# Top-k attention and an MLP mixer: the mask of head 0's last 192 columns goes in among the second scores, and the shared PSUM bank is split evenly

## The chip, the cores and the metric

The kernel runs on one core of one Trainium2 chip. The metric is device time in microseconds (us): the median of three runs before the change was 724.96 us (724.28 to 725.15). One further execution was taken with the hardware profiler; all rows shown here come from it.

## The reference

Eight batches of eight heads, 576 rows, head dimension 64. For each row only the 32 largest scores keep their weight:

```
scores = scale * q @ k^T                       # 576 x 576 for each head
kth    = the 32nd largest score of each row
scores = where(scores >= kth, scores, -1e9)
attn   = exp(scores - max) ; attn /= sum(attn) + 1e-9
x      = heads of attn @ v side by side        # 8 x 576 x 512
h      = relu(x^T @ w_tok1) @ w_tok2           # over the 576 rows
u      = x + h^T
out    = u + relu(u @ w_ch1) @ w_ch2
```

## The kernel before

**Tiles and engines.** Two heads are handled together (`front`, `back`, L450 and L738), in 32 such pairs. The 576 rows of a pair make four tiles of 128 and one of 64, which it shares with the next pair, so two pairs make nine tiles and the whole kernel 144 calls of `scores` (L553), one for each row tile with its two heads: head 0 lives on partitions 0 to 63 of the transposed `qT` and `kT`, head 1 on 64 to 127. For one such call:

- TensorE (PE) computes the scores of both heads, `score` (L569, matmuls at L565). ScalarE (ACT) copies them out of PSUM to `SX` as scaled integers (L598, recorded at L366).
- VectorE (DVE) finds candidates for the 32nd largest with MAX8 over six segments (L614 to L620). ACT counts how many scores lie above a guess (L632). GpSimd (POOL) and DVE turn that into the exact threshold (L640, L649).
- In 100 of the 144 calls (`swap`) POOL writes a mask byte for each score into `U` (L658). Then `rescore` (L577) has PE put mask times a tiny factor into PSUM (`excess`, L583, with `identN` as the stationary operand) and add the scores a second time on top (`second`, L589), so that one ACT instruction (L663) can take the exponential straight out of PSUM. In the other 44 calls POOL multiplies instead (L669, L673).
- `Pm` is transposed by DMA into `PT` (L695), and PE multiplies it with `v` (L754). The mixer follows batch by batch on PE and ACT (`mlp_ops`, L793; L892 and L940 are its largest matmuls).

**PSUM of one call.** The 2 x 576 f32 scores take three banks of 512 columns. Head 0 has bank 0 and the first 64 columns of bank 1, head 1 the last 64 columns of bank 1 and bank 2: `APART = 960` is the distance of the heads, `CUT` (L292) cuts head 0 at 512 and head 1 at 64.

**Row tiles.** A 64-row stationary operand uses one half of the PE array; head 0's matmuls run in one half (row tile 0) and head 1's in the other (row tile 1) at the same time. The kernel never lets the two write the same bank at once. `pieces` (L381) issues four pieces: head 1's first 64 columns (bank 1), head 0's first 512 (bank 0), head 1's last 512 (bank 2), and, behind a wait of PE on the semaphore `tiles_done` until head 1's first piece is complete, head 0's last 64 (bank 1). `score` goes through it once and `rescore` twice, first with `excess`, then with `second`. Each `excess` piece is two matmuls of 64 x 64, one for each half of the rows, so that both row tiles work on it; each `second` piece is one matmul of 64 x 128. A float32 matmul stands in the trace as two instructions.

**The order.** The whole program is a list of 6,041 operations (`plan.add`). `Plan.run` (L206) sorts them by the string `ORDER` (L32), which gives each its place, and issues each engine's own in that order; an engine's queue is not rearranged at run time. The costs in `plan.add` (`dur`, `dma`, `fly`) only choose buffers and banks, and place dummy matmuls (`heat`, L1078) where the plan sees PE idle.

Of the kernel before, what the change touches and what calls it, by code (L numbers as in the profile page):

```python
# [8 lines left out]
P = 128  # L9
# [23 lines left out]
    "$I%M%V%S%U']&Q'^+7+/,$-B1#1,###)$(#$#%#&#'#.#(#0#2$H#*#+#-#_#^#b#a#[#/#4#1#8#6#7#3#9#?#:#;#A#D#F#I#<#=#>#@#B#C#E"  # L33
    '#H#J#5#G#K#P#M#L#S#N#W#e#g#O#U#T#R#Q#V#d#h#j#l$/$-$,$.$4$9$<$B$D$C$N$Q$E$G$F$T$V$c%J%W%u%{&H%K%L%]%_&F#X#Y#f#}#|'
    "#n#q#r$#$%$5#c$$#m#p#w#u$7$:$>#]#`#i#v#z#~#{#s$8$=$A#k#x#o$&#y#t$6$;$O$S$]$_$^$`$t%'%3%P%Q%T%`%d%N%O%R%h%j%l&J&K"
    "&Y&[&x&L&O&n&w&y$0$3$R$r$u$l$W$g$z%$%&$?$x$d$@$y${$}%#%)%?%+%>%=%F%A%H%Y%X%Z&-&4&9&<&>&U&W&T&X&{'i(5(I$J$M$h%%$j"
    "$|$i$n%/%8%:$U%4%*$q%1$w%7%@%G$1$K$e%9$~%6$p$m%B%E%a$P%.$s%5$v$k%D%I%c%e%w%z%y%x&%&+&.&M&S&P&^&a&N&V&R&j','2'T'U"
    "'`'c(k'V'Y'h(C(n$Y$b%,%-%q%f&&&$&0&2&7%0%~%p%i%2%}&)&6&=$X$[$f%m&#%(%n%o&3&5&@$o&'%k%t&,%r&/&;&B&E&u&q&t&r'''&'+"
    "'S'X'W'j'm'R'['Z'p's'{(8(9(e(g(m(:(;),)7*$*3*K*M$'$*#,$2$Z$L$a#Z$)&I(l&o&p&s&v,*%[%^&(&1&_&l&*&A'.'0'6%g&c'(&`'/"
    "&:'3':'?%;%<%b'>'*'9'8&e'B'E'K%C&i'-&8&h%s'7'D'N'Q'e'd'b'f(*(#(1(=(?(<(V(`(@(>(A(c(s(u):);)B)G*&)=)>)y){*'%v%|&?"  # L40
    "&C'4'<&d&D'l'o'q&b'@'C';'1'5'F'n'w&Z&]&f'G')&k'L'O'k'x'~&g'A&m'J't'I'z(%(((.(G(E(D(F(W(T(b)2)0)1)J)L)4)/)3)N)P)R"
    "*(***2*B*i*)*-*4*E*j&}'#'H'M($(,'u(0(6(H(U'=(-(/()(3(4(O(Q(X'$([(j(i(p(})%)@)<)?)m)u*9*<*=*>*?*@*A*k+.+E+H&~'%'}"
    "(Y(K(L(+(^(r(w({'P(&(2(a(_(q(v(|)$'_'a'r(7(Z'v(R(J(y)#)''y'|(N(M('(P(o(~)))+)E)D)H)F)[)b)h*0*1*.*I*N*+*,*/*R*U*b"
    "+2+5+k+n+u+8+9+v+y,j'g(B(])O(x)])a)W)d)n)q(S)V)T)S)M)*)X)l)s(d(h(t)`)g)f)Z)&)o)t)v(z)Y)_)()U)^)e)i*5*8*C*D*F*G*X"
    '*`*{+1+0+3+B+D+4+:+6+J+L+N+r+s+x+~,l+t,&,@,B,k,x-6-9(f)8*o*s+l+o-K-P)x)|*v+)+w+z-T-W.6.G.5.F.O.U/z0M.D.T/4/9/3/:'
    '.Q.V0T0~0U0{0a0}1U241V262k2l2{2x3F3r8.4@5O5[5K5L5]8t&z$+-Y).)-)6)5.>&G&|*%*m*l*q*p,_)9)A)Q*J*Q)p*6)r*[*_*c)K*7*]'
    ")k*H*e*h*x*|)C)I)c*Y*P*V*;*S*^*f*~)j*W)w*O*T*L*g*y+$+&+*+-+,+++I+e+h+q,',%,1,7,),+,(,<,D,G,`,a,s,y-X,f,i-S-V-Z)z"
    ')}*}+G+K+F+;+A+P+S+X*:*d*z*a+%*Z+=+W+[*n*r*w+>+U+C+?+#+Y+]+_+<+R+@+O+Q+T+V+Z+a+c+|,#+}+{,?,N,[,b,c,e-)-4,g,h,d-7'
    "-<-@-E-F-U.8.}-G-H.7.J.~*t+'+^,/,6,4+d,5,:,>,H+b+i,0,8,3,9,=,F,J+p,M,u,t,}-$-.-C-D-A.&.(.,...2.?.A.@.B/#/5/^/a*u"
    "+(+f,L+g,.,],Y,|-#-&+M,W,2,I,E+`,Z,~-++j+m,K,U,{,S,^,V-'-,-/,,,R,--%,O,;-(-*-1-3-Q-M-L-R-q-o-y.9.;.=.`.h.:.C.<.s"  # L50
    '.w.|/-/./d/q/t///0/v/y0Y,A,C,P,Q-?--,T-]-b-d-t,X-h-2-`-g-:-j-r-x,w,z-5-k-a-;->-=-s-w-|-8-i-f-l-n-m-v-z-~.%.M.K.I'
    '.H.q.c.p/+/,/*/B/J/(/1/)/L/Q/S/f/h/|0Q0Z/j/l0P0S0[1F1]1`*#)~/%,n,o,q,p/o,m-[2h.E.P.L.S3p,r,v-_.).4.$-c.1.Z.].a-0'
    ".'.X.0-^-u._.d.m-I-N.+.^.[.W.3.Y.g.l.r-e-}./.*.#-{.e.i.v.y/8/7/</;/O/V/Z/e/i/k0204/m/g/n070:0=1$1&1H1L281%1N2327"
    "2f-J-O.-/M/F.x.f.b/P/T/[-p.z/K/G.k/R/U/`0$.N.R.j/Y/D.t/X.u/_/b0'.n.{/C/I.o/E/]0&0)0+0]0R0^0N0d0m0o1'1)1(14171+1-"
# [206 lines left out]
def kernel(  # L261
# [11 lines left out]
    nc = tc.nc  # L273
# [101 lines left out]
    def row(s, h, lo, hi, p=0, n=P, apart=APART):  # L375
        return bank[p : p + n, s + apart * h + lo : s + apart * h + hi]
# [893 lines left out]
```

## Time and profile before

| | |
|---|---|
| median of 3 runs | 724.96 us (724.28 to 725.15) |
| profiled execution | 724.09 us, span 722.3 us |
| mean granted TensorE clock | 0.993 |
| busy: DVE, ACT, POOL | 661.9, 656.4, 638.0 us |
| dummy matmuls (L1080) | 92 with `identB` at 398 ns, 9 with `warm` |

A row of the groups reads: line, engine, operation, output and inputs, shape, count, then busy us and mean ns of one, then idle time of the engine just ahead of them and what ended it. PE is the matmuls, PEld the loads of stationary operands, which run beside them; the end of a matmul is modelled, its start is not. In the time line a row is a start, a length and a run of like instructions. The chain is the work that ended last, followed back from the end. The granted clock was 0.96 in 40 to 80 us and in 120 to 160 us and 1.00 between 160 and 680 us.

### The profile page before, as it was taken

The page shows a single profiled execution, that of the slowest core. Times are in us where ns is not written, and L with a number is a line of the kernel's source. Part 1 is how long each engine was busy: PE and PEld are TensorE (multiplying, and loading weights), DVE is VectorE, ACT ScalarE, POOL GpSimd, SP SyncE. Part 2 cuts the span into 40 slices and gives each one's busy share as a digit, 9 for nine tenths or more (in the row PEclk, how much of TensorE's full clock was granted, in tenths as well). Part 3 has the DMA queues.
Part 4 walks back from the last instruction along what each step waited for, and adds up shares of the span by engine and source line. Part 5 has one row for each costly group of instructions (what it writes and reads, how often), then busy time and mean ns, then how long its engine had stood idle before and what let it go on. Part 6 is the DMA issues. An engine that isn't in the chain of part 4 may idle for free.

```text
span 722.3 us, 22349 instructions
## 1 busy us (share of the span) xinstructions
PE 690.4 (96%) x7438; PEld 418.6 (58%) x7517; DVE 661.9 (92%) x3812; ACT 656.4 (91%) x1134; POOL 638.0 (88%) x867
## 2 busy tenths in 40 slices
PE   8889989989999999999999999999999999999995
PEld 4445656556566555655665566555565655665652
DVE  7989999989999999999999999999999999997341
ACT  6979999989999999999999999999999999997450
POOL 3997988979999999999999999999999999999400
PEclk9999999999999999999999999999999999999999
DMA  5577889777985759466667565855777737663521
GB/s 134 98 133 128 147 117 151 152 102 128 140 167 124 158 84 181 101 114 138 119 141 145 122 125 107 154 108 124 152 122 157 152 74 154 108 133 72 126 54 63
DMA packets 286715, 90.45 MB, mean 125 GB/s; under 512 B 273024, under 2 KB 283136, under 8 KB 286592
## 3 DMA queue, kind: packets, MB, share of 16 engines
q1 hardware_dynamic: 282768, 84.97, 60.8%
q0 software_dynamic: 3024, 3.77, 3.8%
q8 instruction: 61, 1.00, 0.6%
q14 instruction: 62, 0.51, 0.2%
q10 hardware_dynamic: 800, 0.20, 0.1%
HBM read 35.85 MB, written 9.44 MB: 63 GB/s over the span
## 4 chain that ended last, share of the span: by engine, by line
PE 47%; DVE 28%; POOL 9%; ACT 7%; DMA 4%; issue 3%; SPq 1%; ACTq 0%; POOLq 0%; DVEq 0%
DVE cd L614 13%; PE bank L892 10%; PE bank L565 8%; PE bank L589 8%; DVE tlo L649 8%; PE bank L940 8%; PE bank L754 3%; PE bank L583 3%; POOL SX L640 3%; DMA PT<-Pm 3%; POOL U L658 2%; ACT sg L632 2%; DVE cd L618 2%; POOL Pm L673 2%; ACT SX L366 2%
## 5 line engine op out<-in xcount | busy, mean ns | idle before, releaser
L614 DVE MAX8 cd<-SX 128x8 f32<-128x96 f32 x1728 | 347.6, 245 | 7.1 <-ACT SX L366 6.8
L640 POOL TENSOR_SCALAR SX<-SX,nh,gs 128x576 int32<-128x576 f32 x288 | 235.8, 826 | 12.5 <-DVE gs L710 7.6
L632 ACT ACTIVATE sg<-SX,nh 128x576 bf16<-128x576 f32 x288 | 225.8, 805 | 1.6 <-DVE nh L710 0.7
L649 DVE MAX8 tlo<-SX 128x8 uint32<-128x584 uint32 x288 | 218.2, 758 | 6.0 <-POOL SX L643 3.6
L366 ACT ACTIVATE SX<-bank 128x1152 f32<-128x1152 f32 (+2 forms) x147 | 163.6, 1136 | 12.5 <-PE bank L565 11.2
L658 POOL TENSOR_SCALAR U<-SX,nt,ws 128x576 uint8<-128x576 int32 x200 | 163.6, 829 | 12.4 <-DVE nt L710 8.3
L565 PE MATMUL bank<-kT,qT 64*64 64x64 f32 (+1 forms) x2304 | 168.1, 415 | 5.3 <-ACT SX L366 1.6
L565 PEld LDWEIGHTS bank<-kT,qT 64*64 64x64 f32 x2304 | 85.4, 133 | 94.6 <-issue 40.3
L589 PE MATMUL bank<-kT,qT 64*128 64x64 f32 (+1 forms) x800 | 135.3, 452 | 0.0
L663 ACT ACTIVATE Pm<-bank 128x1152 bf16<-128x1152 f32 x100 | 114.5, 1151 | 12.0 <-PE bank L589 11.5
L673 POOL TENSOR_TENSOR Pm<-E,M 128x576 bf16<-128x576 bf16 x88 | 111.5, 1281 | 2.1 <-DMA PT<-Pm 1.3
L589 PEld LDWEIGHTS bank<-kT,qT 64*128 64x128 f32 x800 | 89.3, 187 | 32.0 <-issue 24.4
L892 PE MATMUL bank<-wc2b,H 128*128 128x512 bf16 x357 | 86.8, 379 | 2.4 <-issue 1.4
L940 PE MATMUL bank<-UT,wc1b 128*128 128x512 bf16 x351 | 86.7, 380 | 2.1 <-issue 1.0
L669 POOL TENSOR_SCALAR M<-SX,no,ws 128x576 int8<-128x576 int32 x88 | 72.6, 829 | 1.8 <-DVE no L731 1.4
L632 ACT ACTIVATION_READ_ACCUMULATOR sg<-SX,nh 128x1 f32 x288 | 65.8, 228 | 0.0
L754 PE MATMUL bank<-vb,PT 128*128 128x65 bf16 x1600 | 55.2, 194 | 3.6 <-DMA PT<-Pm 3.4
L754 PEld LDWEIGHTS <-PT 128*128 128x128 bf16 x1600 | 52.1, 98 | 8.7 <-DMA PT<-Pm 4.0
L583 PE MATMUL bank<-U,identN 64*64 64x512 bf16 (+1 forms) x800 | 53.4, 299 | 3.8 <-ACT SX L366 1.3
L625 ACT ACTIVATE E<-SX,lift 128x1152 bf16<-128x1152 f32 x44 | 56.9, 1296 | 0.0
L892 PEld LDWEIGHTS <-H 128*128 128x128 bf16 x384 | 34.9, 98 | 36.5
L940 PEld LDWEIGHTS <-wc1b 128*128 128x128 bf16 x380 | 34.3, 98 | 36.2
(124 smaller groups left out, 843.0 us busy)
## 6 DMA issues: line engine op xcount, KB each, us to landing
vL<-in_v_dram SPq DMA_DIRECT2D x64, 128.0 KB, 2.5
kL<-in_k_dram SPq DMA_DIRECT2D x63, 128.0 KB, 3.1
qL<-in_q_dram SPq DMA_DIRECT2D x62, 128.0 KB, 3.0
out_dram<-ob SPq DMA_DIRECT2D x14, 512.0 KB, 4.2
PT<-Pm SPq DMA_TRANSPOSE x143, 3.6
wc1b<-in_moe_w_ch_dram POOLq DMA_DIRECT2D x4, 384.0 KB, 5.3
wc2b<-in_moe_w_ch_dram POOLq DMA_DIRECT2D x4, 384.0 KB, 5.5
kL<-in_k_dram SPq DMA_DIRECT2D x32, 32.0 KB, 2.8
```

Of the source, the lines that this page charges most:

```text
L366: return nc.scalar.activation(out=dst, in_=src, func=AF.Copy, scale=GRID, bias=-LEVEL * GRID)
L565: yield nc.tensor.matmul(out=row(s1.t, h, lo, hi, c, 64, apart), lhsT=x["qT"].t[r, q0 : q0 + 64], rhs=x["kT"].t[r, lo:hi], start=True, sto ...
L589: yield nc.tensor.matmul(out=row(s2.t, h, lo, hi), lhsT=x["qT"].t[r, q0 : q0 + P], rhs=x["kT"].t[r, lo:hi], start=False, stop=h == 0 or lo ...
L614: ss.append(plan.add("DVE", 0.06 + (bounds[a + 1] - bounds[a]) / 960, lambda a=a, h=h, cd=cd: nc.vector.max(cd.t[:, a, :], Sb.t[:, h, boun ...
L632: got.append(plan.add("ACT", 0.761, lambda i=i0 + 1 - h, h=h, sg=sg: nc.scalar.activation(out=sg.t[:, :], in_=Sb.t[:, h, 0:S], func=AF.Sig ...
L640: xo.append(plan.add("POOL", 0.805, lambda i=i0 + 1 - h, h=h: nc.gpsimd.tensor_scalar(out=xi(Sb)[:, h, 0:S], in0=Sb.t[:, h, 0:S], scalar1= ...
L649: mxs.append(plan.add("DVE", 0.674, lambda i=i0 + 1 - h, h=h: nc.vector.max(tlo[:, at(i) - 7 : at(i) + 1], Sb.t[:, h, :].bitcast(u32)), [d ...
L658: us.append(plan.add("POOL", 0.805, lambda i=i0 + 1 - h, h=h: nc.gpsimd.tensor_scalar(out=byte(U.t[:, h, :], 1), in0=xi(Sb)[:, h, 0:S], sc ...
L673: oe.append(plan.add("POOL", 1.262, lambda h=h, M=M: nc.gpsimd.tensor_tensor(out=Pm.t[:, h, 0:S], in0=E.t[:, h, :], in1=M.t[:, :], op=ALU. ...
L754: nc.tensor.matmul(out=oo, lhsT=PT[g][0].t[:, 5 * h + j, :], rhs=vb.t[:, j, h, :], start=(j == 0), stop=(j == 4))
L892: nc.tensor.matmul(out=po, lhsT=H.t[:, fc, r0 : r0 + P], rhs=wc2b[:, fc, :], start=(fc == 0), stop=(rows is not None and fc == NF - 1))
L940: nc.tensor.matmul(out=o, lhsT=wc1b[:, cc, fc * P : (fc + 1) * P], rhs=UT.t[:, cc, :], start=(cc == 0), stop=(cc == (hi if whole else NC) ...
```

## The change

Three things are changed.

1. The cut. `APART` becomes 704 and a row starts 128 columns into its first bank: head 0 has 384 columns in bank 0 and 192 in bank 1, head 1 has 192 in bank 1 and 384 in bank 2. `score` issues the same four pieces in the same order, with one wait, in these new sizes. The very first call, which uses four banks and two parts, is cut at 384 as well.
2. The mask. For three of the four pieces `excess` is as before. Head 0's last 192 columns get no `excess` piece; a new function `shared` adds their mask in between the second scores, as two matmuls of 64 x 128 in bf16, one in each row tile, each at a moment when its row tile has bank 1. `rescore` has one wait where it had two.
3. The list. `ORDER` is fitted anew, for changed costs: `rescore` 1.5 to 1.53, and the flight times of DMAs: loads of q and k 1.0 to 1.6, of v 1.2 to 1.6, the transposes 0.6 to 1.3. Nearly all of the 6,041 operations have another place (96%), half of them by no more than 8; on PE 62% stand at another rank, on average by 1.5.

```diff
-    CUT, APART = ((0, SM, S), (0, ST, S)), 2 * SM - ST
+    APART = 704
+    HS = SM - P
+    CUT = ((0, HS, S), (0, S - HS, S))
...
     def pairs(s):
-        o = APART - S if s else 0
-        return bank[:, s - o : s - o + 2 * APART].rearrange("p (h c) -> p h c", h=2)[:, :, o : o + S]
+        return bank[:, s + P : s + P + 2 * APART].rearrange("p (h c) -> p h c", h=2)[:, :, 0:S]
...
+    def count(o, group):
+        o.then_inc(tiles_done, 1)
...
+    def hold():
+        nc.tensor.wait_ge(tiles_done, done[0])
...
         def score():
-            pieces(score_piece)
+            for o in first(1, 0):
+                count(o, f"first{i0}")
+            list(first(0, 0))
+            list(first(1, 1))
+            hold()
+            *_, o = first(0, 1)
...
+            def shared(a):
+                r = slice(64 * a, 64 * a + 64)
+                return nc.tensor.matmul(
+                    out=row(s2.t, 0, HS, S), lhsT=identN[r, :], rhs=U.t[r, 0, HS:S], start=False, stop=False)
...
-            pieces(excess)
-            pieces(second)
+            group = f"second{i0}"
+            excess(1, 0)
+            excess(0, 0)
+            excess(1, 1)
+            count(shared(1), group)
+            count(second(1, 0), group)
+            second(0, 0)
+            second(1, 1)
+            hold()
+            shared(0)
+            tc.declare_fence(second(0, 1).ins, group=group)
```

In `excess(h, part)`, `second(h, part)` and `first(h, part)` the head `h` is 0 or 1 and the part the first or second of its two; `shared(1)` and every `second(1, ..)` are row tile 1, `shared(0)` and every `second(0, ..)` row tile 0.

More of the change, by code (lines that the diff above doesn't have):

```diff
@@ L38 @@
[L38 to L42, printed above, removed]
@@ L141 @@
+    "eleoeeekemegeneseiepeqewf#eue}etezeve~f<f=fCfDebf?f@fAfEf5f6f7f;f'f(f2f4f%f&f+f0f3erf/f1f8f9f:f>fB"
 )
@@ L371, in pairs @@
     def pairs(s):
[L372 to L373 removed]
+        return bank[:, s + P : s + P + 2 * APART].rearrange("p (h c) -> p h c", h=2)[:, :, 0:S]
     def row(s, h, lo, hi, p=0, n=P, apart=APART):
[L376 removed]
+        return bank[p : p + n, s + P + apart * h + lo : s + P + apart * h + hi]
     tiles_done = tc.alloc_semaphore("tiles_done")
     done = [0]
[L381 to L392 removed]
+    def count(o, group):
+        o.then_inc(tiles_done, 1)
+        tc.add_to_no_dep_group(group, o.ins)
+        tc.no_tile_sem_insts.add(o.ins.name)
+        done[0] += 1
+    def hold():
+        nc.tensor.wait_ge(tiles_done, done[0])
     prog = tc.manual_schedule()
@@ L559, in scores, with first @@
         ts = [x[w] for x, _ in sides[: 2 - whole] for w in ("qT", "kT")]
-        def score_piece(h, lo, hi, apart=APART):
+        def first(h, part, apart=APART):
             r = slice(64 * h, 64 * h + 64)
+            lo, hi = CUT[h][part : part + 2]
             for a, (x, q0) in enumerate(sides):
@@ L569, in score, with score_part @@
         def score():
-            pieces(score_piece)
-        def score_part(part):
-            for h in range(2):
-                for _ in score_piece(h, CUT[0][part], CUT[0][part + 1], 2 * SM):
-                    pass
+            for o in first(1, 0):
[4 more added lines that the diff above has]
+            *_, o = first(0, 1)
+            tc.declare_fence(o.ins, group=f"first{i0}")
+        def score_part(lo, hi):
+            for h in range(2):
+                r = slice(64 * h, 64 * h + 64)
+                for a, (x, q0) in enumerate(sides):
+                    nc.tensor.matmul(
+                        out=row(s1.t, h, lo, hi, 64 * (a ^ h) if swap else 64 * a, 64, 2 * SM),
+                        lhsT=x["qT"].t[r, q0 : q0 + 64], rhs=x["kT"].t[r, lo:hi], start=True, stop=True)
@@ L577, in rescore, with excess @@
         def rescore():
             x, q0 = sides[0]
-            def excess(h, lo, hi):
+            def excess(h, part):
+                lo, hi = CUT[h][part : part + 2]
                 for a in range(2):
                     r = slice(64 * a, 64 * a + 64)
-                    yield nc.tensor.matmul(
+                    nc.tensor.matmul(
                         out=row(s2.t, h, lo, hi, 64 * (a ^ h), 64), lhsT=identN[r, r],
-                        rhs=U.t[r, h, lo:hi], start=h == 1 or lo == 0, stop=False)
@@ L587, in second @@
-            def second(h, lo, hi):
+                        rhs=U.t[r, h, lo:hi], start=True, stop=False)
+            def shared(a):
+                r = slice(64 * a, 64 * a + 64)
+                return nc.tensor.matmul(
+                    out=row(s2.t, 0, HS, S), lhsT=identN[r, :], rhs=U.t[r, 0, HS:S], start=False, stop=False)
+            def second(h, part):
                 r = slice(64 * h, 64 * h + 64)
-                yield nc.tensor.matmul(
+                lo, hi = CUT[h][part : part + 2]
+                return nc.tensor.matmul(
@@ L661, in weights @@
                         [on, ow], acq=[U] if h else [], use=[U, Sb, nt, ws]))
-                orr = plan.add("PE", 1.5, rescore, us, acq=[s2, Pm], use=[U] + ts, mode=(1, 2))
+                orr = plan.add("PE", 1.53, rescore, us, acq=[s2, Pm], use=[U] + ts, mode=(1, 2))
                 oe = [plan.add("ACT", 1.013, lambda: nc.scalar.activation(
```

238 lines of the change are left out of this document (115 added, 123 removed).

## The prediction

> **What bounds the kernel now.** I read the page first: its engines and the chain that ended last, then that chain line by line.
>
> ```profile
> span 722.3 us, 22349 instructions
> PE 690.4 (96%) x7438; PEld 418.6 (58%) x7517; DVE 661.9 (92%) x3812; ACT 656.4 (91%) x1134; POOL 638.0 (88%) x867
> PE 47%; DVE 28%; POOL 9%; ACT 7%; DMA 4%; issue 3%; SPq 1%; ACTq 0%; POOLq 0%; DVEq 0%
> by line: DVE cd L614 12.5%; PE bank L892 10.5%; PE bank L565 8.5%; PE bank L589 8.3%; DVE tlo L649 8.2%; PE bank L940 7.8%; PE bank L754 3.1%; PE bank L583 3.0%; issue 2.9%; POOL SX L640 2.8%; DMA PT<-Pm 2.7%; POOL U L658 2.4%; ACT sg L632
> ```
>
> PE carries half of the chain. The lines that the change touches, L565, L583 and L589, are 8.5, 3.0 and 8.3% of it. The stretches by window (columns: us, then PE, PEld, DVE, ACT, POOL busy and counts, clock, DMA) say how much room the others leave; below them L589 alone in the last two stretches, and the chain between 574 and 714 us:
>
> ```profile
> 40.00:240.00 200.00, 188.87 (x2175) 118.45 (x2186) 192.22 (x1126) 187.79 (x317) 181.61 (x254) 0.98 0.80 138
> 240.00:574.00 334.00, 326.94 (x3603) 199.24 (x3641) 329.83 (x1934) 330.81 (x577) 328.22 (x438) 1.00 0.67 131
> 574.00:676.00 102.00, 100.79 (x1000) 59.90 (x1014) 91.95 (x491) 91.94 (x162) 99.62 (x134) 1.00 0.52 103
> ...
> 574.00:676.00 102.00, 21.53 (x128) 14.20 (x128) 1.00 0.52 103
> 676.00:722.30 46.30, 1.35 (x8) 0.89 (x8) 0.96 0.32 84
> ...
> by line: PE bank L892 25.9%; PE bank L940 18.4%; PE bank L589 14.9%; PE bank L565 11.0%; PE bank L754 6.7%; PE bank L583 5.5%; PE bank L853 2.5%; PE bank L474 2.5%; PE bank L926 1.9%; PE bank L897 1.8%; PE bank L818 1.7%; PE bank L833 1.4%;
> ```
>
> From 574 us on the chain's parts are all PE's: what PE saves there is saved. Between 240 and 574 us all four engines are busy; DVE rests 334.0 - 329.8 = 4.2 us, so a faster PE can shorten this stretch by no more. Between 40 and 240 us DVE rests 7.8 us.
>
> **One rescore today.** The time line of PE and of its weight loads, with the shapes' means:
>
> ```profile
> 301.35 1.20 PE L565 MATMUL bank<-kT,qT 64*64 64x64 f32 x16
> 302.37 0.55 PE L583 MATMUL bank<-U,identN 64*64 64x512 bf16 x8
> 302.86 1.34 PE L589 MATMUL bank<-kT,qT 64*128 64x64 f32 x8
> 304.65 0.52 PE L583 MATMUL bank<-U,identN 64*64 64x64 bf16 x8 [0.45 <-ACT SX L366]
> 305.10 1.35 PE L589 MATMUL bank<-kT,qT 64*128 64x64 f32 x8
> 306.38 0.66 PE L565 MATMUL bank<-kT,qT 64*64 64x64 f32 x6
> ...
> 302.33 0.17 PEld L583 LDWEIGHTS <-identN 64*64 64x64 bf16 x4
> 302.71 0.11 PEld L583 LDWEIGHTS <-identN 64*64 64x64 bf16 x2 [0.21 <-PE bank L583]
> 302.85 0.73 PEld L589 LDWEIGHTS bank<-kT,qT 64*128 64x128 f32 x7
> ...
> L565 PE MATMUL bank<-kT,qT 64*64 64x512 f32 x1152 | 164.4, 603 | 0.2 <-DVE kT L533 0.2
> L589 PE MATMUL bank<-kT,qT 64*128 64x512 f32 x400 | 134.6, 632 | 0.0
> L565 PE MATMUL bank<-kT,qT 64*64 64x64 f32 x1152 | 81.9, 228 | 5.0 <-ACT SX L366 1.6 <-ACT kT L548 1.1 <-ACT qT L546 1.0
> L583 PE MATMUL bank<-U,identN 64*64 64x64 bf16 x400 | 43.0, 210 | 3.1 <-ACT SX L366 1.3 <-ACT Pm L663 1.2
> L583 PE MATMUL bank<-U,identN 64*64 64x512 bf16 x400 | 42.9, 389 | 0.7 <-POOL U L658 0.7
> ...
> L589 PEld LDWEIGHTS bank<-kT,qT 64*128 64x128 f32 x800 | 89.3, 187 | 32.0 <-issue 24.4
> L565 PEld LDWEIGHTS bank<-kT,qT 64*64 64x64 f32 x2304 | 85.4, 133 | 94.6 <-issue 40.3 <-PE bank L565 26.7 <-ACT SX L366 5.1
> L754 PEld LDWEIGHTS <-PT 128*128 128x128 bf16 x1600 | 52.1, 98 | 8.7 <-DMA PT<-Pm 4.0 <-issue 0.6
> L583 PEld LDWEIGHTS <-identN 64*64 64x64 bf16 x800 | 28.7, 105 | 34.5 <-PE bank L583 16.9 <-issue 4.4 <-ACT Pm L663 4.2
> ```
>
> The unit prices are differences of these means, since a constant tail stands in each. A bf16 column costs (389 - 210) / 448 = 0.40 ns, an f32 column (603 - 228) / 448 = 0.84 ns in each of its two recorded halves. An f32 load of 128 columns is 187 - 133 = 54 ns longer than one of 64, so I put 0.054 us on 64 and 0.108 on 128; a bf16 load of 64 is 28 ns shorter than the f32 one, 0.026 us.
>
> The mask phase takes 302.37 to 302.86, 0.49 us, behind a score, and 304.65 to 305.10, 0.45 us, from a standstill. Head 1's 576 columns stream in 576 x 0.40 = 0.23 us. The rest is the wait: the load of head 0's last piece starts at 302.71, though the 64 columns it waits for streamed in 0.026 us from 302.37. From their end to the released load there are 0.34 - 0.026 = 0.31 us. The weight loads lost 16.9 us to it (group of L583, `PE bank L583`).
>
> The second phase takes 305.10 to 306.38, 1.28 us. Head 1's two halves of 64 columns (54 ns each) are shorter than the 0.108 us load of the next stationary operand, so it is three loads, 0.32, and 2 x 512 x 0.84 = 0.86, together 1.18 us. The 0.10 left over is the change of array shape; 0.09 lies likewise ahead of the second phase (the held load at 302.71, plus 0.026 for the load and 0.026 for its columns, ends at 302.76; the next load starts at 302.85). This phase's own wait costs nothing: head 1's first piece streams to 0.108 + 0.108 + 0.054 = 0.27, its release at 0.27 + 0.31 = 0.58 comes before row tile 0 has done its 512 columns, at 0.108 + 0.86 = 0.97.
>
> **The change, part by part.**
>
> The wait inside the mask phase goes. What is late next is head 1's 0.23 us: 0.026 + 0.23 + 0.09 = 0.35 instead of 0.45 from a standstill, and 0.02 to 0.04 more is gained behind a score, where the first load is hidden. I take -0.105 us.
>
> The second phase gets two bf16 matmuls of 192 columns and one hold. Call the bf16 load of 64 x 128 L. Row tile 1: L, then the next load 0.108 (longer than 192 x 0.40 = 0.08), then 2 x 576 x 0.84 = 0.97 without gaps, since 192 columns (0.16) now cover a load: 1.07 + L. Row tile 0: 0.108 + 2 x 384 x 0.84 = 0.75, then `shared(0)`, as long as the load behind it, 0.108, then 2 x 192 x 0.84 = 0.32: 1.18. Both stay at 1.28 with the shape change, if the hold doesn't delay row tile 0. The hold is over when `second(1, 0)` is complete, streamed to L + 0.108 + 0.32. Add 0.31 as the only hold that makes PE wait in this trace shows, or 0.16 at least (a 64-column bf16 matmul is recorded as 210 ns, of which load and columns are 52), and the load L itself: `shared(0)` starts at 2L + 0.59 to 2L + 0.74, and isn't late up to 0.75.
>
> No row shows a bf16 load of 64 x 128. Nearest are the 64 x 64 one, 0.026, doubled 0.052, and the full 128 x 128 one of L754, whose 50 matmuls with their loads pass in 1.53 us, at most 0.031 each:
>
> ```profile
> 299.82:301.35 1.53, 1.53 (x50) 1.47 (x49) 1.00 0.04 11
> ```
>
> Between 0.031 and 0.052 the delay is 0 to 0.09 us; I take 0.035. Net, a rescore gets 0.07 us shorter (0.105 at best, 0.015 at worst), on 100 rescores 7 us of PE's queue (1.5 to 10.5). Behind the hold only `shared(0)`, `second(0, 1)` and the next operation's loads are queued; the ACT exponential waits for the last.
>
> [...]
>
> `score` keeps its columns: per row tile one load and 576 x 2 x 0.84 = 0.97, together 1.02, as 301.35 to 302.37 shows. Its hold comes later, since head 1's first piece is 192 columns: 0.054 + 0.32 + 0.16 to 0.31, a load of 0.054 behind it, 0.59 to 0.74, against 0.054 + 0.64 = 0.70 when row tile 0 needs it. I cost it at nothing; at worst it is 0.04 on each score.
>
> The first call: ACT's first copy shrinks from 512 to 384 columns and starts earlier, but head 0's copy comes behind the same 1,152 columns. Nothing.
>
> The new list can't be costed by rows. What it aims at are PE's stalls on landings:
>
> ```profile
> PE bank L754 <- DMA PT<-Pm: 3.4, 3, 1.7
> PE bank L474 <- DMA kL<-in_k_dram: 2.5, 1, 2.5
> ```
>
> Four stalls, each given some 0.65 us more (flight 0.6 or 0.7 higher), are 2.6 us; with PE's 47% of the chain 1.2. A new order can lose elsewhere, so I take a third, -0.4, and hold 3 us either way for possible: all 5.9 us of these stalls at 47% are 2.8. On SP's queue the loads stand earlier in the list (those of v by 17 places on average) and the output's stores later (115), which lets a load land sooner and delays no reader in the kernel.
>
> **The sum.** L589's share of the chain is 8.3% of 722.3 = 60 us, at 1.28 each 47 rescores. Of these, 17 lie behind 574 us (128 and 8 instructions, 8 to a rescore): 17 x 0.07 = 1.2 us, in full. The 30 ahead of it save 2.1 us, of which I take half, 1.05, because DVE, ACT and POOL have so little rest there. With the list 0.4: 2.65 us. The profiled execution goes from 724.09 to 721.4; the median stood 0.87 above it, so 724.96 - 2.65 = 722.3 us.
>
> **The rivals.**
> - *The saving turns into waits.* PE finishes earlier but DVE, ACT and POOL set the pace up to 640 us, and in the tail the mixer of the last batch waits for the last exponentials anyway. For it: the 4.2 us of DVE rest in 334. Against it: the unbroken PE chain from 574 us. At most half of the tail's 1.2 remains: 724.4.
> - *The hold becomes the bound.* If the bf16 load is as slow as the f32 one, L = 0.108 and `shared(0)` starts at 0.81 to 0.96, 0.06 to 0.21 late; the gain of 0.105 is eaten when it is 0.105 late, at L = 0.058 with the 0.31 us that the trace shows. Net up to 0.10 longer, in the middle 0.06, on 47 rescores 2.8 us: 727.8. For it: the f32 row. Against it: both bf16 load rows.
> - *The list loses.* PE's queue is in order; two or three more stalls like the 1.7 us one in the stretches where PE is the chain, less the 2.25 gained: 726.1 to 727.8, say 727.0. Against it: only a few places' moves on PE.
> - *More than that is gained.* All 47 rescores at 0.105, 4.9 us, and the list's 2.8: 718 as the end.
>
> **How the numbers follow.** A measurement of this kernel can tell about 0.2%, 1.45 us, from no change: the same is 723.5 to 726.4. Forecast 0.45, more gained 0.13, turned into waits 0.20, hold 0.10, list 0.12. So faster 0.58, same 0.20, slower 0.22. The range 718.0 to 728.0 holds all but the outer half of the gain case and the upper ends of the two losses.
>
> **What would show it.** In the changed profile: from the first mask matmul to the first second-score matmul 0.31 to 0.36 us instead of 0.45 to 0.49; the idle row of the mask loads behind PE gone or moved to `shared`; the second phase 1.28 to 1.35 us; scores still 1.02. The forecast is wrong if the second phase is over 1.38 (hold), if the phases shrink and the span doesn't (waits: then idle time of PE ended by ACT, POOL or DVE grows by some 5 us), or if PE's stalls on landings grow (list).

## The result, and the profile after

The changed kernel takes 712.50 us (median of 4 runs, 711.75 to 713.98), the kernel before 724.89 (4 runs, 724.28 to 725.15): ratio 0.9833, 95% interval 0.9814 to 0.9851. That is 12.4 us less where the prediction had 2.65, and below its range. The profiled execution took 711.75 us with a span of 709.8, so 12.5 us of span went. In the kernel after, the lines of before are 23 higher (L614 is L637, L754 is L777); of the rescore's lines L583 is L591, L589 is L603, L565 is L563, and the new one is L597.

Page of the kernel after: busy times, then the chain by engine and by line:

```profile
PE 687.3 (97%) x7516; PEld 442.6 (62%) x7516; DVE 661.7 (93%) x3812; ACT 653.7 (92%) x1134; POOL 635.2 (89%) x867
DVE 60%; ACT 17%; PE 15%; POOL 3%; issue 3%; DMA 1%; ACTq 0%; POOLq 0%; DVEq 0%
```

PE had 47% of the chain and now has 15%; DVE went from 28 to 60%. Busy times hardly changed, so the span lost idle time, not work. Where, the stretches show (columns as before):

```profile
40.00:240.00 200.00, 194.56 (x2277) 129.93 (x2272) 199.75 (x1187) 194.48 (x333) 190.16 (x266) 1.00 0.80 143
240.00:574.00 334.00, 329.74 (x3662) 214.18 (x3660) 331.53 (x1938) 332.63 (x580) 328.84 (x439) 1.00 0.68 131
574.00:676.00 102.00, 101.68 (x1086) 64.52 (x1085) 81.00 (x426) 84.78 (x150) 89.24 (x120) 1.00 0.53 111
```

Between 40 and 240 us DVE rested 7.8 us before and rests 0.25 now: 7.5 of the 12.5 us, in the stretch to which the prediction gave almost nothing. The granted clock there went from 0.98 to 1.00. Between 240 and 574 us DVE's rest went from 4.2 to 2.5 us. Another 2.5 us of it went in the first 10 us, but that part need not be the change's: over the profiles of all runs DVE's rest there lies between 2.5 and 5.2 us, with the old tiles and with the new.

The part that the prediction did cost came as it said. One rescore in the time line, first PE, then the weight loads:

```profile
307.99 0.43 PE L591 MATMUL bank<-U,identN 64*64 64x192 bf16 x6
308.35 0.25 PE L597 MATMUL bank<-U,identN 64*128 64x192 bf16 x1
308.36 0.92 PE L603 MATMUL bank<-kT,qT 64*128 64x384 f32 x5
309.11 0.24 PE L597 MATMUL bank<-U,identN 64*128 64x192 bf16 x1
309.12 0.58 PE L603 MATMUL bank<-kT,qT 64*128 64x384 f32 x3
309.64 1.20 PE L563 MATMUL bank<-kT,qT 64*64 64x192 f32 x16
...
308.35 0.09 PEld L597 LDWEIGHTS <-identN 64*128 64x128 bf16 x1 [0.22 <-issue]
308.35 0.63 PEld L603 LDWEIGHTS bank<-kT,qT 64*128 64x128 f32 x6
309.02 0.09 PEld L597 LDWEIGHTS <-identN 64*128 64x128 bf16 x1
```

The mask phase lasts from 307.99 to 308.35, 0.36 us instead of 0.45 to 0.49. The second phase lasts to 309.64, 1.29 us instead of 1.28, although two more matmuls and a hold stand in it. Over all 100 rescores the median of the mask phase went from 0.452 to 0.365 us and that of the second phase from 1.277 to 1.285. The wait of the mask loads on PE (L583, 16.9 us in all) has no counterpart: at the hold the loads of `shared(0)` idle 0.03 us each. The 0.22 us ahead of the load of `shared(1)` passes while the mask's columns stream.

### The profile page after: what moved, and what is told of

It reads as the page before. It is cut to its first block, busy times and chain, and to the rows that moved or that the text cites. A ratio compares the mean times of both kernels' runs of the same rounds, so it can differ in the third digit from the quotient of the medians.

```text
span 709.8 us, 22355 instructions
## 1 busy us (share of the span) xinstructions
PE 687.3 (97%) x7516; PEld 442.6 (62%) x7516; DVE 661.7 (93%) x3812; ACT 653.7 (92%) x1134; POOL 635.2 (89%) x867
## 4 chain that ended last, share of the span: by engine, by line
DVE 60%; ACT 17%; PE 15%; POOL 3%; issue 3%; DMA 1%; ACTq 0%; POOLq 0%; DVEq 0%
DVE cd L637 26%; DVE tlo L672 18%; ACT sg L655 6%; PE bank L915 4%; DVE cd L641 4%; ACT SX L368 4%; PE bank L963 3%; DVE thi L643 3%; DVE m L640 2%; DVE Xb L794 2%; ACT Pm L686 2%; PE bank L603 2%; ACT E L648 2%; PE bank L563 2%; ACT H L1008 2%
## 5 line engine op out<-in xcount | busy, mean ns | idle before, releaser
L637 DVE MAX8 cd<-SX 128x8 f32<-128x96 f32 x1728 | 348.9, 245 | 1.9 <-ACT SX L368 1.6
L655 ACT ACTIVATE sg<-SX,nh 128x576 bf16<-128x576 f32 x288 | 229.8, 841 | 2.4 <-DVE nh L733 1.9
L563 PE MATMUL bank<-kT,qT 64*64 64x192 f32 (+1 forms) x2288 | 167.4, 413 | 7.9 <-ACT SX L368 4.1
L368 ACT ACTIVATE SX<-bank 128x1152 f32<-128x1152 f32 (+2 forms) x147 | 166.4, 1166 | 4.9 <-PE bank L563 2.8
L563 PEld LDWEIGHTS bank<-kT,qT 64*64 64x64 f32 x2288 | 103.3, 132 | 61.6 <-ACT SX L368 10.4
L603 PE MATMUL bank<-kT,qT 64*128 64x384 f32 (+1 forms) x800 | 134.6, 423 | 0.0
L603 PEld LDWEIGHTS bank<-kT,qT 64*128 64x128 f32 x800 | 93.2, 188 | 0.2
L915 PE MATMUL bank<-wc2b,H 128*128 128x512 bf16 x384 | 90.8, 380 | 0.0
L963 PE MATMUL bank<-UT,wc1b 128*128 128x512 bf16 x380 | 89.6, 379 | 0.3 <-DVE Xb L794 0.3
L655 ACT ACTIVATION_READ_ACCUMULATOR sg<-SX,nh 128x1 f32 x288 | 76.1, 264 | 0.0
L777 PEld LDWEIGHTS <-PT 128*128 128x128 bf16 x1600 | 51.6, 98 | 6.9 <-issue 5.4
L777 PE MATMUL bank<-vb,PT 128*128 128x65 bf16 x1600 | 54.7, 194 | 0.3 <-ACT SX L368 0.2
L1008 ACT ACTIVATE H<-bank 128x512 bf16<-128x512 f32 x88 | 53.8, 713 | 0.8 <-PE bank L963 0.7
```

The costliest lines, as they stand in the source:

```text
L368: return nc.scalar.activation(out=dst, in_=src, func=AF.Copy, scale=GRID, bias=-LEVEL * GRID)
L563: yield nc.tensor.matmul(out=row(s1.t, h, lo, hi, c, 64, apart), lhsT=x["qT"].t[r, q0 : q0 + 64], rhs=x["kT"].t[r, lo:hi], start=True, sto ...
L603: return nc.tensor.matmul(out=row(s2.t, h, lo, hi), lhsT=x["qT"].t[r, q0 : q0 + P], rhs=x["kT"].t[r, lo:hi], start=False, stop=h == 0 or p ...
L637: ss.append(plan.add("DVE", 0.06 + (bounds[a + 1] - bounds[a]) / 960, lambda a=a, h=h, cd=cd: nc.vector.max(cd.t[:, a, :], Sb.t[:, h, boun ...
L655: got.append(plan.add("ACT", 0.761, lambda i=i0 + 1 - h, h=h, sg=sg: nc.scalar.activation(out=sg.t[:, :], in_=Sb.t[:, h, 0:S], func=AF.Sig ...
L915: nc.tensor.matmul(out=po, lhsT=H.t[:, fc, r0 : r0 + P], rhs=wc2b[:, fc, :], start=(fc == 0), stop=(rows is not None and fc == NF - 1))
```

## The experiments

All ratios are to the kernel before, run on the same chip beside them. A landing is the moment at which the data of a DMA has arrived. From e5 on theory A says that the new list gains by sparing three landings for which PE waited in the first 160 us, and theory B that its gain lies in the fit of thousands of places. In e1 to e4b the question was still whether list or tiles gave the gain at all, and the letters mean what the expectation of e1 says: A the list, B the 0.08 us saved on each rescore, C both together. The changes of order below are given in short, not as code.

| run | ratio (95% interval) | time, before beside it |
|---|---|---|
| e1 list and costs alone | 0.9890 (0.9853 to 0.9927) | 716.19, 723.59 |
| e2 tiles alone | 0.9961 (0.9932 to 0.9989) | 722.74, 723.59 |
| e4 after, 0.08 us back per rescore | 0.9851 (0.9815 to 0.9888) | 713.69, 723.59 |
| e4b after, 0.16 us back | 0.9925 (0.9888 to 0.9962) | 718.88, 723.59 |
| e5 three moves | 1.0041 (1.0024 to 1.0058) | 726.79, 724.49 |
| e6 new list to place 2120 | 0.9965 (0.9947 to 0.9983) | 721.40, 724.49 |
| e7 DVE's order alone | says nothing (below) | 3941.09, 724.49 |
| e8 all but DVE's order | 1.0191 (1.0164 to 1.0218) | 738.00, 724.49 |
| e10 three moves, shorter | 1.0029 (1.0012 to 1.0045) | 726.65, 724.66 |
| e11 one load moved | 0.9978 (0.9950 to 1.0007) | 723.51, 724.66 |
| e12 as e10, new tiles | 1.0000 (0.9982 to 1.0019) | 724.07, 724.66 |
| e13 after, load late again | 0.9859 (0.9835 to 0.9884) | 713.84, 724.66 |
| e14 moves that keep DVE's order | 0.9950 (0.9929 to 0.9972) | 720.75, 724.34 |
| e15 as e14, new tiles | 0.9918 (0.9888 to 0.9947) | 717.89, 724.34 |
| e16 as e14, fewer dummies | 0.9930 (0.9914 to 0.9947) | 719.19, 724.72 |
| e17 as e15, fewer dummies | 0.9906 (0.9888 to 0.9924) | 717.42, 724.72 |
| e18 as e13, fewer dummies | 0.9875 (0.9840 to 0.9910) | 713.22, 724.72 |
| e19 after, no dummies behind 45 us | 0.9874 (0.9855 to 0.9893) | 715.54, 724.72 |

**List or tiles: e1 and e2.** e1 is the kernel before with the new `ORDER` and its costs, e2 the new tiles with the old `ORDER` and the old costs.

```diff
 e1:  -ORDER = (old)   +ORDER = (new)     and the five changed costs; tiles as before
 e2:  tiles of the change                 ORDER and costs as before
```

> The kernel before (its cut, its two mask waits) with the new list and the new costs. Theory A, the list took DVE's waits away: 714 to 717 us, DVE idle between 40 and 240 us under 3 us. Theory B, the 0.08 us saved on each of 100 rescores carries the gain: 722 to 726, mask phase 0.45 to 0.48 us and DVE idle in that stretch still 6 us or more. Theory C, the list only pays with the shorter rescore: 718 to 724.

> The new cut and the mask among the second scores, with the old list and the old costs. A: 721 to 723 us, the forecast's own estimate for the rescores. B: 712 to 716. C: 719 to 723. In all of them the mask phase is 0.355 to 0.365 us and the second phase 1.28.

The list alone gives 1.1% (some 8 us), the tiles alone 0.4% (2.8 us). Both times lie where A had them. So the tiles gave about what the forecast had for them, 2.25 (e2's interval allows 0.8 to 4.9), and the list twenty times its 0.4. Together with the new tiles the list is worth 1.28% (e2 against the kernel after), some 9 us. DVE's busy time between 40 and 240 us was 192.22 before; e1's row, then e2's:

```profile
40.00:240.00 200.00, 194.72 (x2269) 121.38 (x2262) 198.53 (x1173) 192.93 (x330) 189.20 (x263) 1.00 0.80 142
```

```profile
40.00:240.00 200.00, 187.45 (x2150) 125.87 (x2150) 189.49 (x1104) 184.27 (x312) 179.35 (x252) 0.97 0.77 135
```

e2's profiled execution was its longest (726.19; its ten runs lie between 717.43 and 726.19), so its waits may be larger than in most executions of that kernel. Its rescores are the shorter ones, and yet DVE is 2.7 us worse off than before. The waits of that stretch (us in all, times, the longest) show where; e2, then the kernel before:

```profile
DVE gs L733 <- ACT sg L655: 5.3, 3, 3.6
PE bank L777 <- DMA PT<-Pm: 4.9, 3, 2.4
DVE cd L637 <- ACT SX L368: 3.6, 2, 3.4
PE bank L471 <- DMA kL<-in_k_dram: 3.5, 1, 3.5
```

```profile
DVE cd L614 <- ACT SX L366: 3.1, 3, 2.6
DVE gs L710 <- ACT sg L632: 2.8, 1, 2.8
DVE rds L768 <- PE bank L754: 0.7, 1, 0.7
```

PE waits 5.9 us for landings in the kernel before and 8.4 in e2. Counted from the issue of the transfer, PE comes 0.4 and 1.2 us sooner to the first two landings in e2 and 0.1 later to the third, and the first and third transfers take 0.6 and 0.8 us longer. So of the longer waits some 1.5 us are the faster PE's and the rest the transfers' own. And DVE's waits stand 0.6 to 8 us behind PE's, as the time line of the kernel before shows, the first landing and DVE's answer to it, and DVE's answer to the third:

```profile
46.86 0.48 PE L474 MATMUL bank<-identF,kL 128*128 128x128 f32 x1 [2.53 <-DMA kL<-in_k_dram]
...
52.76 0.42 DVE L614 MAX8 cd<-SX 128x8 f32<-128x96 f32 x2 [2.55 <-ACT SX L366]
...
162.31 0.17 DVE L710 TENSOR_SCALAR gs<-cnt 128x12 f32<-128x12 f32 x1 [2.77 <-ACT sg L632]
```

PE waited 2.53 us for k of pair 3 (to 46.86), 1.66 for `PT` of pair 2 (to 94.37), and 1.20 and 0.51 for `PT` of pair 4 (to 153.52 and 154.51). DVE idled 2.55 us at 52.8, 0.70 at 95.0, 2.77 at 162.3.

**The tiles' time put back: e4, e4b.** The kernel after, with a first `excess` piece of head 1 issued once more than needed; the rescore is 0.08 us longer, as it was before the change, and in e4b 0.16.

```diff
+            excess(1, 0, True)      # e4; in e4b excess(1, 1, True): first once with stop=True
             excess(1, 0)
             excess(0, 0)
```

> The changed kernel with head 1's first mask piece issued twice, which puts about 0.08 us back into each of 100 rescores and changes nothing else. A: 713 to 715 us, since other engines cover it. B and C: 717 to 721, 0.6 to 1 us for each us of TensorE time.

> The changed kernel with head 1's 384-column mask piece issued twice, some 0.16 us more in each rescore, 16 us of TensorE's queue. A: 715 to 719 us. B and C: 723 to 729. If the first 0.08 costs less than the second, the changed kernel has slack on TensorE that the kernel before did not have.

The first 8 us of PE's queue (100 rescores of 0.08) cost 1.2 us, which is not clear of noise, since e4's interval overlaps that of the kernel after; the next 8 us cost 5.2. Both times lie in A's ranges. In the kernel after DVE sets the pace and PE has some room; the room is used up by the first 8 us, and the chain turns back to PE (15% in the kernel after, 57% in e4, 66% in e4b). Taking the tiles away altogether costs more, 4.1 us (e1 against the kernel after, by their ratios). Why this is more than e4's 1.2 stays open; the intervals of e1 and e4 overlap.

**Parts of the list: e6, e7, e8.** All on the kernel before, with the old costs; where the merged places would break a dependence, the later operation waits its turn. e6 takes the first 2,120 of 6,041 places (to some 235 us) from the new list; e7 only DVE's order, up to there; e8 every engine's but DVE's, up to place 1700.

```diff
-ORDER = (old)
+ORDER = (e6: new to place 2120, then old | e7: DVE's new, others' old | e8: DVE's old, others' new)
```

> The kernel before, with the first 2120 of the 6041 places of the list from the new list (some 235 us of the span) and the rest in the old order. Theory A (the gain of the list lies where the landings were late, in the first 160 us): all but 1 or 2 us of what the whole new list alone gained, so 716 to 718 beside 724. Theory B (gain spread over the whole list): about a third of it, 720.5 to 722.

> The kernel before, with only VectorE's order taken from the new list, up to place 2120; PE, SP, ScalarE and GpSimd keep the old order. Theory A (late landings on PE, a matter of SP's and PE's order): the three waits of PE on landings stay at 1.2 to 3.5 us and the time stays within 1.5 us of the kernel before. Theory B (VectorE's own order was the flaw): VectorE's busy time in 40 to 240 us comes near 198 of 200, and the time falls by 4 us or more.

> The kernel before, with the order of every engine but VectorE taken from the new list, up to place 1700 (some 190 us). Theory A: the waits of PE on landings are gone and the time falls by 4 to 7 us. Theory B (VectorE's own order was the flaw): less than 2 us.

e8 is 13.5 us slower and e7's main part ends 30 us later: one engine's order doesn't fit the other engines' from another list, and neither run could tell the theories apart. e7's time says nothing more. The program ends with a test of its own figures and, where that fails, computes all of it again by an exact path; it did so here from 756 us on, for a reason that is not shown. e6 came out where B had it, -0.35%. It is read best by the lead of one and the same milestone, the start of the n-th of the 1,728 MAX8 of candidates, against the kernel before (us; worked out from the traces; e10 to e16 are described below):

| n (at, in before) | 100 (36) | 200 (72) | 300 (109) | 400 (147) | 500 (189) | 700 (262) | 1000 (375) | 1600 (602) |
|---|---|---|---|---|---|---|---|---|
| after | 1.1 | 3.1 | 4.3 | 4.3 | 8.4 | 9.6 | 9.9 | 11.6 |
| e1 | 0.9 | 2.9 | 4.1 | 4.4 | 7.1 | 7.6 | 7.7 | 8.7 |
| e6 | 1.7 | 3.7 | 4.9 | 5.2 | 7.8 | 5.9 | 5.2 | 4.9 |
| e2 | -1.3 | -2.2 | -4.1 | -4.0 | -4.0 | -3.5 | -3.1 | -2.5 |
| e10 | 0.3 | 2.2 | -3.7 | -3.9 | -1.5 | -0.7 | -0.7 | -0.4 |
| e14 | -1.0 | 0.8 | 0.5 | 1.4 | 2.7 | 3.5 | 3.6 | 3.1 |
| e15 | -1.9 | 0.1 | 0.1 | 1.0 | 3.4 | 4.7 | 5.1 | 6.0 |
| e16 | 0.4 | 3.1 | 3.2 | 4.0 | 3.7 | 4.0 | 4.1 | 4.3 |

n = 100 lies ahead of the first landing, so what stands there differs by the start alone. e1's lead then comes in steps: 2.0 behind the first landing, 1.2 behind the second, 2.7 behind the third, and 1.6 more by n = 1600. e6 has all of it at 189 us and loses 2.6 by 375 us, behind the place where the old order takes over. So most of the list's gain comes in the first 190 us. That e6 shows little of it because the two orders don't fit at the seam is likely but not shown.

**The landings, first tries: e5, e10, e12, e11.** On the old list: the load of k of pair 3 goes one place ahead of that of q of pair 5 (needed 45 us later); the products of attention and `v` of pairs 2 and 4 (L754; PV2 and PV4 below) go behind a score and, in e5 for both and in e10 for pair 4 only, a rescore. e12 is e10 on the new tiles with the old costs; e11 moves the load alone.

```diff
 SP:  load q5, PT, load k3          ->  load k3, load q5, PT        (all four)
 PE:  PV2, score, rescore           ->  score, rescore, PV2         (e5);  score, PV2, rescore (e10, e12)
 PE:  PV4, score, rescore           ->  score, rescore, PV4         (e5, e10, e12)
```

> The kernel before, tiles and costs as they were, with three instructions of the old list moved: the load of k of pair 3 one place ahead of the load of q of pair 5 on SP, and the PV products of pairs 2 and 4 one score and one rescore later on PE. These are the three places at which PE waited for a landing (2.5, 1.7 and 1.7 us) and after which the granted clock was halved twice for 3.4 us. Theory A (the new list gains because it takes these three waits away, and the clock drops with them): the three waits are gone or under 0.5 us each, no slice of the granted clock before 600 us is under 0.9, VectorE's busy time in 40 to 240 us grows by 3 us or more from 192.2, and the time falls by 4 to 8 us, to some 716 to 720 beside 724. Theory B (the whole list is fitted anew, and its gain is spread over thousands of places): the waits go, but the time falls by less than 2 us, since what PE waits less, VectorE waits for something else.

> The kernel before with three instructions of its old list moved, as in the run with three moves, but the PV products of pair 2 only one score later (there they were a score and a rescore later, so that the mixing step behind them, L818, made PE wait 4.7 us for Xb and VectorE 6.0 us). Theory A (in the kernel before VectorE idles 2.55 us at 52.8, 0.70 at 95.0 and 2.77 at 162.3 us, right behind the three landings for which PE waited 2.53, 1.66 and 1.20 + 0.51 us; the new list gains by sparing these): of the 6.0 us some 4 go and nothing takes their place, VectorE's busy time in 40 to 240 us is 196 or more, and the time falls by 3 to 5 us. Theory B (the gain of the new list is in the fit of thousands of places): VectorE's time goes up by less than 2 us, and the time falls by less than 1.5 us, or not at all.

> The row tiles of the change with the old list and the old costs (722.7 us beside 723.6 of the kernel before), and the three moves of the first run of this set. There PE waits 3.55, 2.41 and 1.95 us for the three landings and VectorE idles 3.42, 1.13 + 1.51 and 3.64 us behind them. Theory A: some 6 us of VectorE's idle time goes, and the time falls to 715 to 718 beside 724, within 2 to 5 us of the change with its own list. Theory B: 720 or more.

> The kernel before with one move: on SP the load of k of pair 3 goes one place ahead of the load of q of pair 5, which is needed 45 us later. Theory A: PE's wait of 2.53 us at 46.9 us is gone or under 0.7, VectorE's 2.55 us at 52.8 shrink to 0.7 or less, and the time falls by 1.2 to 2.2 us. Theory B: less than 0.7 us.

Theory A failed in e5, e10 and e12 as it was put: no landing was waited for any more, and the time rose or stayed. The waits of e10 between 90 and 120 us show the reason:

```profile
DVE gs L710 <- ACT sg L632: 6.4, 2, 5.7
ACT H L823 <- PE bank L818: 4.7, 1, 4.7
PE bank L818 <- DVE Xb L771: 4.6, 1, 4.6
```

With the products of pair 2 moved down the list, DVE's step that reads them (L768, L771) fell behind some 35 DVE instructions that had stood after it. The mixing step (L818) waited 4.6 us for `Xb`, the granted clock fell to 0.50 for 6.8 us, and DVE waited 5.7 us for what came after. The lead shows both: 2.2 at n = 200, behind the first landing; 5.9 lost by 300, the edit's own; 2.4 won by 500, behind the third. e11 shows the load alone: its wait is gone and DVE's 2.55 us are 0.7, but PE then waits 1.92 us instead of 1.66 at the second landing, and DVE's waits there are 1.10 and 1.27 instead of 0.70 and those behind the third 3.1 instead of 2.8. In this profile what was won at one landing was waited away at the next two. Its median is 0.22% shorter, with an interval that reaches no change; this run can't tell A from B.

**The landings with DVE's order kept: e14 to e17.** Scores and a rescore go ahead of the PV products, within PE's order only; DVE's, ACT's and POOL's stay word for word.

```diff
 SP:  load q5, PT, load k3          ->  load k3, load q5, PT
 PE:  PV2, score                    ->  score, PV2
 PE:  PV4, score, rescore           ->  score, rescore, PV4
 e16, e17 besides:
+    FEW = {173: 2, 687: 0, 971: 0, 1309: 0, 1378: 0}
...
-                    for j in range(... int(0.8 * (st - t0 - 0.1) / d)):
+                    for j in range(... min(int(0.8 * (st - t0 - 0.1) / d), self.FEW.get(o.n, 99))):
```

> The kernel before with five instructions of its old list in another order and nothing else: on SP the load of k of pair 3 ahead of the load of q of pair 5; on PE one score ahead of the PV products of pair 2, and one score and one rescore ahead of those of pair 4. VectorE, ScalarE and GpSimd keep their order. Theory A (the landings): PE's waits of 2.53, 1.66 and 1.20 + 0.51 us on landings shrink to under 0.8 each, VectorE's 2.55, 0.70 and 2.77 us behind them to under 1 each, no new wait of over 1.5 us comes up, and the time falls by 3.5 to 5.5 us, which is about half or more of what the whole new list gave alone (8 us). Theory B (thousands of places): less than 1.5 us.

> The row tiles of the change with the old list and the old costs (0.996 of the kernel before), and the same five instructions in another order. There PE waited 3.55, 2.41 and 1.95 us for the three landings. Theory A: these waits are under 1 us each and the time falls to 715 to 718.5 beside 724 (ratio 0.987 to 0.992). Theory B: 0.994 or more.

> The kernel before with the five instructions in another order (720.75 us beside 724.34), and the dummy matmuls ahead of five PE operations held to what the kernel before has there, so that 101 or fewer are left instead of 118. If the extra dummies took PE time that the chain needed, the time falls by another 1.5 to 3.5 us, to 717 to 719: then the landings account for 5 to 7 of the list's 8 us. If they only filled waits, it stays within 1 us of 720.75: then more than half of the list's 8 us is the fit of the other places.

> The same on the row tiles of the change with the old list and the five instructions in another order (717.89 us beside 724.34). If the extra dummies cost: 714.5 to 716.5. If they only filled waits: within 1 us of 717.9.

With eight queue positions in another order, five on PE and three on SP, the kernel before gains 0.50%, 3.6 us (e14), and the new tiles 0.43% (e15 against e2). Both times lie at the weak end of A's ranges, and two of DVE's waits are still over the 1 us that A allowed in e14. The plan sees PE idle ahead of the moved instructions and puts 17 more dummy matmuls there, 4.9 us of PE's time by the trace. Held to 98 in all (101 in the kernel before), the gain is 0.70%, some 5 us (e16), of the list's 1.1%. That the dummies cost anything is not shown: e14's and e16's intervals overlap, 719.2 lies between the two ranges expected for e16, and e17 is within 0.5 us of e15, as expected if they only filled waits. Waits of e14 and of e16 between 40 and 240 us:

```profile
DVE gs L710 <- ACT sg L632: 1.7, 2, 1.3
DVE rds L768 <- PE bank L754: 1.2, 1, 1.2
PE bank L754 <- DMA PT<-Pm: 0.7, 2, 0.5
```

```profile
DVE gs L712 <- ACT sg L634: 3.2, 2, 2.6
PE bank L756 <- DMA PT<-Pm: 2.2, 3, 1.0
```

The 5.9 us of PE's waits on landings are 0.7 and 2.2. e16 follows e1's lead to n = 400 (3.1, 3.2, 4.0 against 2.9, 4.1, 4.4) and falls behind it by 3.4 at 500: it meets the third landing earlier than e14 and still waits there, DVE 2.6 us behind it. e14 and e15 hardly wait there (PE 0.55 us and 0.3). From n = 400 to 500 they win 1.3 and 2.4 us, where e1 and the kernel after win 2.7 and 4.1. So on the old tiles the landings account for 3.6 (e14) to 5 us (e16) of the list's 8. On the new tiles e17 has 0.94% and the kernel after 1.67; of that list's gain of 1.28%, more than half (0.73) is not accounted for by these moves. What gives the rest, B's fit or some other wait, stays open.

**The late load put back: e13, e18.** The kernel after, with the load of k of pair 3 behind that of q of pair 5; e18 also without the dummies that the plan adds there.

```diff
 SP:  PT, load k3, load q5          ->  PT, load q5, load k3
```

> The kernel after with one swap in its list: the load of k of pair 3 goes behind the load of q of pair 5 on SP, as the old list had it. Theory A: PE waits again some 2 to 3.5 us for that landing near 46 us, the granted clock falls there, VectorE idles 2 us or more behind it, and the time is 1.5 to 3 us longer than the kernel after (ratio to the kernel before 0.986 to 0.988 instead of 0.983). Theory B: within 0.7 us of the kernel after.

> The kernel after with the load of k of pair 3 behind that of q of pair 5 (713.84 us, 1.3 longer than the kernel after), and without the seven dummies that the plan puts in the longer wait that it sees there. If that run was longer because of the late load: 713 to 714.5 and a wait of PE of 1.5 us or more near 46 us. If it was longer because of the dummies (2 us of PE): 712 to 713, as the kernel after.

e13's wait came to 0.5 us, not the 2 to 3.5 that A expected, and the dummies that the plan adds filled part of the place; without them (e18) PE waits 1.0 us. Both are longer than the kernel after by 0.3 to 0.4% of the time before, with intervals that overlap its own. The new list's other places already bring that load earlier, so one swap doesn't restore the wait. These two runs help neither A nor B.

**Without dummies: e19.**

```diff
-    WARM, LIT, FIRST = 2000.0, 0.5, 9
+    WARM, LIT, FIRST = 45.0, 0.5, 9
```

> The kernel after without the 53 dummy matmuls behind 45 us (some 20 us of PE's time). If they fill waits only and the granted clock stays at 1.00 without them: 710.5 to 713, no difference to the kernel after. If they keep the clock up: the clock falls to a half for some microseconds at several places between 45 and 240 us and the time rises to 714 or more.

3.0 us longer than the kernel after: the granted clock falls to 0.50 around 46 us and 156 us, and PE waits for a landing again, 2.5 us. The dummies pay. The lead puts the loss at the third landing: 4.1 at n = 400, where the kernel after has 4.3, and 4.5 at 500, where it has 8.4. Whether the lower clock or the returned wait costs more is not separated.

## Why the prediction was wrong

**The mask phase**: right. Forecast 0.35, measured 0.36. The saving was taken as 0.105 and is 0.09.

**The second phase and the hold**: right. Forecast 1.28 plus at most 0.09, taken 0.035; measured 1.29, 0.01 more than before. That the whole rescore came out at 0.08 us against 0.07 is thus two small errors that cancel. L, the unknown, lay below the range it was given; the groups of the kernel after:

```profile
L603 PEld LDWEIGHTS bank<-kT,qT 64*128 64x128 f32 x800 | 93.2, 188 | 0.2
L591 PEld LDWEIGHTS <-identN 64*64 64x64 bf16 x600 | 20.0, 104 | 22.2 <-issue 7.4 <-ACT SX L368 4.8 <-ACT Pm L686 3.0
L597 PEld LDWEIGHTS <-identN 64*128 64x128 bf16 x200 | 18.5, 92 | 24.4 <-issue 21.6
```

The 128-column bf16 load is recorded at 92 ns, less than the 64-column one (104) and half of the f32 one (188). The prediction's own measure, the recorded time less some 79 ns that it takes for a constant tail (105 - 26), makes L 0.013 us, an estimate, where it had 0.031 to 0.052. Of the 24.4 us of idle time 21.6 lie ahead of `shared(1)`, 0.22 each; at the hold there are 2.8 us, and they cost PE nothing (its L597 rows have no idle time).

**The scores**: right, 1.02 us as before.

**What that is worth**: right in size. Forecast 2.25 us for all; measured 2.8 on the old list (e2), 2.9 between e14 and e15, 1.8 between e16 and e17, and 1.2 when taken away again on the new list (e4). The split that the forecast added up, 1.2 us behind 574 us and 1.05 ahead of it, was not tested.

**The list**: here it failed. The step was "with PE's 47% of the chain 1.2. A new order can lose elsewhere, so I take a third, -0.4, and hold 3 us either way for possible: all 5.9 us of these stalls at 47% are 2.8." Measured: 8 us (e1), of which the landings alone give 3.6 (e14) to 5 (e16; by its interval 3.8 to 6.2, above the 2.8 held for the most). Three things in the step were wrong. The stalls were to lose 2.6 of their 5.9 us; in e1 they lost 4.7 (1.2 us of PE's waits on landings are left). A share of the whole span's chain was put on waits that all lie in the first 160 us, as if half of them were hidden there; but DVE, which rests little in that stretch, idled 2.55, 0.70 and 2.77 us behind them, in all 6.0 us for PE's 5.9, and in e1 its rest there fell from 7.8 to 1.5 us. And the wait was taken for its whole price, although the granted clock fell behind two of the three:

```profile
46.00:47.00 1.00, 0.14 (x1) 0.14 (x2) 1.00 (x8) 0.39 (x2) 1.00 (x1) 0.69 1.27 192
47.00:48.00 1.00, 1.00 (x4) 0.39 (x5) 1.00 (x6) 0.63 (x2) 1.00 (x3) 0.50 0.79 58
48.00:49.00 1.00, 1.00 (x4) 0.44 (x3) 1.00 (x11) 1.00 (x2) 0.79 (x1) 0.50 0.00 0
49.00:50.00 1.00, 1.00 (x5) 0.30 (x2) 1.00 (x10) 0.04 (x1) 0.99 (x2) 0.61 0.00 0
...
156.00:157.00 1.00, 1.00 (x18) 0.54 (x10) 1.00 (x8) 0.00 (x0) 1.00 (x3) 0.50 1.22 204
157.00:158.00 1.00, 1.00 (x16) 0.69 (x9) 1.00 (x9) 0.77 (x1) 1.00 (x3) 0.50 0.50 80
```

By the clock's columns it stood at 0.50 for some 3.4 us each time, by which 1.7 us of PE's work are lost, an estimate; the table of before had the trace of it, 0.96 in 40 to 80 and 120 to 160 us. What the slower clock alone cost is not separated by any run. The prediction quoted DVE's 7.8 us of rest in that stretch as room, and did not ask what DVE was waiting for there; 6.0 of them stand behind these landings. What the list gave beyond the landings, some 3 to 4 us of 8 on the old tiles, stays open.

**The rivals.** The saving did not turn into waits on the whole, the hold did not become the bound, the list did not lose. The last rival, more gained, went the right way with its end at 718. The hold's middle price was mis-added: 0.06 to 0.21 us late, less the 0.105 gained, is 0.03 in the middle and not 0.06, so that rival's time was 726.4 and not 727.8.

## What to carry to other kernels

A wait for a landing is priced in the stretch where it lies, with the idle time of the other engines behind it and with the clock that may fall after it, not by an engine's share of the whole chain. When an engine rests in a stretch where it should set the pace, look up what ended each of its rests before calling it room. In a fitted order move an instruction within its own engine's queue, and see which readers a move in the common list takes along.

## What the runs showed of the hardware

- **The granted clock behind PE's waits.** In the kernel before it stood at 0.50 from 46.37 to 49.79 us, from 2.0 us into the wait of 2.53 us on, and from 155.60 to 159.01, 1.1 us behind the second of the waits of 1.20 and 0.51 us, a microsecond apart; behind the 1.66 us to 94.37 it stayed at 1.00. In e16 waits of 1.02 and 0.55 us, again a microsecond apart, were followed by some 3.4 us at 0.50 (151.4 to 154.8). A wait of 1.9 us near 18 us was followed by no fall in e12 and by 3.4 us at 0.50 in e15; first e12, then e15 (columns: us, PE busy, clock, DMA):

```profile
15.26:18.68 3.42, 2.08 (x30) 1.00 0.62 152
18.68:22.09 3.41, 2.77 (x39) 1.00 0.55 125
22.09:25.50 3.41, 3.41 (x30) 1.00 0.71 129
...
14.88:18.29 3.41, 3.41 (x40) 1.00 0.54 140
18.29:21.70 3.41, 1.47 (x24) 1.00 0.62 140
21.70:25.12 3.42, 3.42 (x27) 0.50 0.37 83
```

  PE was idle for 1.34 and 0.64 us of the first two rows of e12 and for 1.94 us of the second of e15. So the length of a wait alone does not tell whether the clock falls: 1.66 and 1.9 us went without a fall, 1.71 in two parts and 1.9 with one.
- **Do landings spread the time?** Not shown. In one set of runs the kernel before and e2, which wait for landings, lie between 720.6 and 727.6 and between 717.4 and 726.2 us, and four runs of the kernel after within 2.2 us; but four runs of the kernel before lay within 0.9 us, and e18, with waits of 1.0 us, spread over 8.3.
- **A 64 x 128 bf16 load in a row tile is short**: 92 ns recorded, against 104 for the 64 x 64 one and 188 for f32.
